# One V slot, a one-pair loop, o turned by the head sums, and thirty small loads in a decode block

## The chip, the cores and the metric

One core of a Trainium2 chip runs the kernel in one launch. The time is device time in microseconds (us). TensorE (PE) does matrix products, VectorE (DVE) and ScalarE (ACT) do elementwise work and reductions, GpSimd (POOL) helps VectorE, and SyncE (SP) issues nearly all transfers, on one queue; 16 DMA engines carry them out.

## The reference: what is computed

A decode step for 2 tokens: layer norm, attention with 32 heads over a cache of 8192 keys and values per head (float32, 128 wide), and a channel-mixing MLP (512 to 1792 to 512).

```python
q = (x @ wq).reshape(B, Sq, H, Dh)...            # x: layer-normed, [2, 1, 512]
scores = jnp.einsum("bhqd,bhkd->bhqk", q, k_cache) * (Dh ** -0.5)
p = _softmax(scores, axis=-1)
o = jnp.einsum("bhqk,bhkd->bhqd", p, v_cache)
h = x + o...reshape(B, Sq, H * Dh) @ wo
h2 = h + gelu(_layernorm(h) @ w1 + b1) @ w2 + b2
```

K and V are 2 x 32 x 8192 x 128 floats each, 268 MB each: nearly all of the 561 MB that the kernel loads, each byte used once.

## The kernel before, in words

**Units and pairs.** A pair g is two heads (16 pairs); a unit is one pair for one token b, so there are 32 units, and unit i = 2g + b. An even unit is the first token of its pair, an odd unit the second. A unit has a K tile and a V tile of 128 partitions x 16384 floats, 8.39 MB each: one half of the partitions for each head, 128 keys per partition.

**What one unit does.** K is multiplied in place by q, which stands broadcast in PSUM, in two chunks of 80 and 48 keys (`multiply`, VectorE); GpSimd folds the products of the first chunk in half (`halve`); VectorE sums them (`add_up`) and takes each partition's maximum (`row_max`). After the odd unit the pair's maxima are brought together (`all_max`), ScalarE computes the exponentials and their sums (`exps`), and TensorE multiplies them with V: `values` for the even V at the end of the odd unit, and for the odd V inside the next even unit. ScalarE copies the sum out (`gather`), and `head_sum` and `head_out` bring it into the form that the output projection needs. So the even V of a pair can only be used when both K tiles of that pair are done.

**Slots and the order of the loads.** Three slots of 8.39 MB (`slot`, a ring) hold all K and V tiles in turn, a new tile always taking the one longest unused. In unit i SyncE issues the V of unit i-1 and then the K of unit i+1 (`load`, L437). A load waits until what was in its slot has been read: V of unit j takes the slot of K of unit j, and K of unit j that of V of unit j-3. SyncE issues in order, so a load that waits holds up all behind it.

**Waits.** `Waits` follows every instruction by the memory that it reads and writes and gives each the semaphore waits that it needs. DMAs are put on 12 semaphores in turn (`LANES`); a DMA waits for the last one on its semaphore. `Rounds` writes TensorE's program of three pairs once and loops over it five times (`GH = 3`, L239 in the profile), the last pair being written out (L191).

**q.** Every third pair, `stage` copies the q of three pairs to partitions 0 to 3 (L417); `make_q` broadcasts one pair's q to 128 partitions in one of three PSUM banks.

**o.** Before, `head_sum` leaves 4 rows of 128 for each pair, `head_out` (L543) scales them into `orow`, which holds three pairs, and after every third pair `turn` transposes these 12 small pieces on TensorE and `turned` adds them into `oall`. The last pairs' o are laid out over 64 partitions chosen by `LEFT`, to fit a part of wo (`wog`) that GpSimd gathers row by row. In the last unit `project_all` multiplies all but the last pair with wo, while the last V is still loading; the last pair and the MLP follow at the end. Seventy-two small matmuls (`SPARE`) run at the start and their result is not used.

Of the kernel before, what the change touches and what calls it, by code (L numbers as in the profile page):

```python
# [12 lines left out]
P = 128  # L13
# [7 lines left out]
SPARE = 72  # L21
GP = 6
GH = 3
SR = 4
LW = 6
LEFT = (((3, 7), (9, 16), (20, 28), (44, 47), (54, 57), (67, 93), (101, 106), (110, 114), (118, 122)),)
# [12 lines left out]
class Waits:  # L39
    LANES = 12  # L40

    def __init__(self, nc):
        self.nc = nc
        self.sems, self.count, self.clock, self.after, self.mem, self.mask = ({} for _ in range(6))
        self.lane = {}
        self.off = False
        nc.push_inst_callback(self.seen)
# [63 lines left out]
    def skip(self, n):  # L111
        self.lane["hard"] += n
# [5 lines left out]
    def place(self, eng, op, areas):  # L118
        areas = [(x, w) for x, w in areas if x is not None]
        queue = (eng,)  # L120
        if "DMA" in op:
            kind = "soft" if eng == "Pool" else "hard"
            k = self.lane.get(kind, 0)
            self.lane[kind] = k + 1
            proc = (kind, k % self.LANES)
        else:
            proc = queue
# [33 lines left out]
    def close(self):  # L161
# [3 lines left out]
        last = ("hard", (self.lane["hard"] - 1) % self.LANES)  # L165
# [80 lines left out]
class Room:  # L246
# [3 lines left out]
    def tile(self, shape, dtype, name, tag=None, bufs=None, ahead=0):  # L250
# [6 lines left out]
        ring.append(ring.pop(ahead))  # L257
        v = ring[-1][:shape[0], :n]
# [6 lines left out]

    def turn(self, key, n):
        ring = self.held[key]
        ring[:] = ring[n:] + ring[:n]


def tile_decode_block(nc, waits, x, k, v, wq, wo, wog, w1, bias, w2, out):
# [10 lines left out]
    GL = NP - 1  # L282
    units = [(g, b) for g in range(NP) for b in range(B)]
# [11 lines left out]
    def slot():  # L295
        return kv.tile([P, ROW], F32, name="kv", tag="kv")
# [7 lines left out]
    wqt = slot()  # L304
# [3 lines left out]
    wgt = wts.tile([P, len(LEFT), SR, D], F32, name="wgt")  # L308
# [8 lines left out]
    orow = const.tile([4, GH, 2, DH], F32, name="orow")  # L317
    oall = const.tile([P, 2, 2 * GP, B], F32, name="oall")
    NQ = len(LEFT)
    og = const.tile([P, NQ * SR + LW - TH, B], F32, name="og")  # L320
    slots = [kept(x) for x in LEFT]
    first_slot = [sum(n for _, n in slots[:q]) for q in range(len(LEFT))]
    HG = H - LW
    NS = (HG - 4 * GP) * DH // SR
    assert sum(n for _, n in slots) == NS
# [3 lines left out]
    pms = {}  # L329
    for x in LEFT:  # L330
        if x not in pms:
            pms[x] = const.tile([P, P], F32, name=f"pm{len(pms)}")
            nc.gpsimd.memset(pms[x], 0.0)
            for p0, s0, n in kept(x)[0]:
                nc.gpsimd.tensor_copy(pms[x][:, p0:p0 + n], ident[:, s0:s0 + n])
    pm = [pms[x] for x in LEFT]
    FAR = 4096.0
    ioff = const.tile([P, len(LEFT)], F32, name="ioff")
    for q in range(len(LEFT)):
        nc.gpsimd.tensor_scalar(ioff[:, q:q + 1], pidx, first_slot[q] - FAR, None, op0=ALU.add)  # L340
# [9 lines left out]
    so2 = [psa.tile([P, 512], F32, name="so"), [psq.tile([P, 512], F32, name="qps") for _ in range(3)][2]]  # L350
# [5 lines left out]
    qs = const.tile([2 * B, GH, DH], F32, name="qs")  # L356
    wz = const.tile([P, B], BF16, name="wz")
    nc.gpsimd.memset(wz, 0.0)
# [9 lines left out]
    y2 = wgt[:B, 0, 0, :]  # L368
    nc.vector.tensor_scalar(y2, x2, mv[:, 0:1], rs, op0=ALU.subtract, op1=ALU.mult)

    ypt = psm.tile([P, DC, B], F32, name="sm")
# [4 lines left out]
    ipt = psm.tile([P, len(LEFT)], F32, name="sm")  # L376
    for q in range(len(LEFT)):
        pe.matmul(ipt[:, q:q + 1], pm[q], ioff[:, q:q + 1], start=True, stop=True)
# [8 lines left out]
    i4 = ident[:4, :4].rearrange("m (b s) -> m b s", s=2)  # L387
    hmask = const.tile([4, 2], F32, name="hmask")
    nc.vector.tensor_add(hmask, i4[:, 0, :], i4[:, 1, :])

    gidx = const.tile([P, len(LEFT)], mybir.dt.int32, name="gidx")
# [13 lines left out]
    QP, S, MX, MT, GM, LT, RL, SS, OP, OT, TP = ({} for _ in range(11))  # L405
# [5 lines left out]
    def stage(m):  # L411
        g = GH * min(m, NP // GH - 1) + 1
        n = next((n for n in range(1, GH) if (g + n) % NG == 0), 1)
        for at, n in ((0, n), (n, GH - n)):
            rows, cols = of_pair(g + at)
            src = q2[rows, cols.start:cols.start + n * DH]
            nc.vector.tensor_reduce(qs[:, at:at + n].rearrange("m k d -> m (k d)"), src[:, :, None], axis=AX.X, op=ALU.max)  # L417

    def make_q(g):
        QP[g] = psq.tile([P, B, DH], F32, name="qps")  # L420
        for b in range(B):
            rows, cols = of_pair(g)
            q = qs[:, (g - 1) % GH, :] if g else q2[rows, cols]
            pe.matmul(QP[g][:, b], pick[:2 * B, b, :], q, start=True, stop=True)

    make_q(0)
    stage(0)
    rowacc = psa.tile([B, D], F32, name="rowacc")
    for _ in range(SPARE):
        pe.matmul(rowacc[:, :B], wz, wz, start=True, stop=True)  # L430

    def load(src, i, parts):
        g, b = units[i]
        t = slot()
        rows = src[b, 2 * g:2 * g + 2].rearrange("h (p j) d -> (h p) (j d)", j=NS2)
        for s0, n in parts:
            nc.sync.dma_start(t[:, s0 * DH:(s0 + n) * DH], rows[:, s0 * DH:(s0 + n) * DH])  # L437
        return t

    def load_wo():  # L440
        t = slot()
        n = (2 * 2 * GP + LW) * D
        t = t[:, ROW - n:]
        nc.sync.dma_start(t, wo)
        for q in range(NQ):
            nc.gpsimd.indirect_dma_start(
                out=wgt[:, q].rearrange("p r n -> p (r n)"), out_offset=None,
                in_=wog,
                in_offset=bass.IndirectOffsetOnAxis(ap=gidx[:, q:q + 1], axis=0),
                bounds_check=NS - 1, oob_is_err=False)  # L450
        tv = t[:, :2 * 2 * GP * D].rearrange("p (j r n) -> p j r n", j=2, n=D)
        return tv, t[:, 2 * 2 * GP * D:].rearrange("p (r n) -> p r n", n=D)

# [24 lines left out]
    def row_max(i):  # L478
        g, b = units[i]
        if not b:  # L480
            MX[g] = work.tile([P, B], F32, name="mx", bufs=3)
            MT[g] = psm.tile([1, B, P], F32, name="sm")
# [3 lines left out]
    def all_max(g):  # L486
        gm = work.tile([1, B, 2], F32, name="gm", bufs=3)
        nc.vector.tensor_reduce(gm, MT.pop(g).rearrange("o b (s p) -> o b s p", s=2), axis=AX.X, op=ALU.max,  # L488
                                negate=True)
        GM[g] = psm.tile([P, B, 2], F32, name="sm")  # L490
# [15 lines left out]
    def total(g):  # L506
        RL[g] = psm.tile([4, 1] if g < GL else [P, 4], F32, name="sm")
        if g < GL:
            pe.matmul(RL[g], lt4, ones[:, 0:1], start=True, stop=True)
        else:  # L510
            pe.matmul(RL[g], ones, lt4, start=True, stop=True)

    def inverse(g):
        r = work.tile(list(RL[g].shape), F32, name="rl" if g < GL else "rlp")
# [17 lines left out]
    def head_sum(g):  # L532
        ss = SS.pop(g)
        OP[g] = psm.tile([4, DH] if g < GL else [P, 2 * B], F32, name="sm")
        for j in range(4):
            sj = ss[:, j * DH:(j + 1) * DH]
            a, w = (sel4[:, :, j], sj) if g < GL else (sj, sel4[:, :, j])
            pe.matmul(OP[g], a, w, start=(j == 0), stop=(j == 3))

    def head_out(g):  # L540
        op, rl = OP.pop(g), RL.pop(g)
        if g < GL:
            nc.vector.scalar_tensor_tensor(orow[:, g % GH], op[:, None, :].to_broadcast([4, 2, DH]), rl,  # L543
                                           hmask[:, :, None].to_broadcast([4, 2, DH]), op0=ALU.mult, op1=ALU.mult)
            return
        nc.vector.tensor_tensor(otz[:, :, 0:B], *(x.rearrange("p (b s) -> p s b", b=B) for x in (op, rl)),
                                op=ALU.mult)

    def turn(j):
        rows = orow.rearrange("m k e d -> m (k e d)")  # L550
        if j < 4:
            TP[j] = psm.tile([HP, 2 * GP, 2 * B], F32, name="sm")
            rows = rows.rearrange("m (p r) -> m r p", r=2 * GP)
            for r in range(2 * GP):
                pe.transpose(TP[j][:, r, :], rows[:, r, :], ident[:4, :4])
            psm.turn("sm", 2)
            return
        TP[j] = psm.tile([P, NQ * SR + LW - TH, 2 * B], F32, name="sm")
        at, n = (HG - 4 * GP) * DH, LW - TH
        last = rows[:, at:at + n * DH].rearrange("m (p r) -> m r p", r=n)  # L560
        for r in range(n):
            pe.transpose(TP[j][:, NQ * SR + r, :], last[:, r, :], ident[:4, :4])
        rows = rows.rearrange("m (s r) -> m r s", r=SR)
        for q, (_, n) in enumerate(slots):
            s0 = first_slot[q]
            for r in range(SR):
                pe.transpose(TP[j][:n, q * SR + r, :], rows[:, r, s0:s0 + n], ident[:4, :4])

    def turned(j):
        if j < 4:  # L570
            tp = TP.pop(j)
            half = slice(HP * (j % 2), HP * (j % 2 + 1))
            nc.vector.tensor_reduce(oall[half, j // 2], tp.rearrange("p r (b s) -> p r b s", b=B), axis=AX.X, op=ALU.add)
            return
# [271 lines left out]
```

## Time and profile before

| | |
|---|---|
| time, median of 2 runs | 1302.81 us (1302.77 to 1302.85) |
| profiled execution, first to last instruction | 1301.3 us (no other time of it is given) |
| bytes loaded | 561 MB, at 431 GB/s over the span |
| busy: VectorE, TensorE, GpSimd, ScalarE | 75%, 30%, 28%, 4% |
| SyncE's queue, share of the 16 engines' time | 99.7% |

The profile is one execution on the chip. A line of a timeline gives start and length in us, engine, line of the kernel, operation and what it writes and reads; brackets give the idle time ahead and what ended it. "SPq" is SyncE's queue: its entries are the moments at which a load is issued, not when it runs. The loads of K and V go by the tensor `kv` for all slots. In a table by windows each engine has its busy time and, in brackets, its instructions.

### The profile page before, as it was taken

To read this page: it belongs to the slowest core of one execution; us is meant where nothing else is said; L and a number is where in the kernel's file an instruction comes from. 1 tells how busy PE (TensorE), PEld (TensorE's weight loads), DVE (VectorE), ACT (ScalarE), POOL (GpSimd) and SP (SyncE) were. 2 spreads that over 40 slices of the span, in tenths; PEclk is the share of its full clock that TensorE was granted. 3 is DMA by queue.
4 is the path that set the end of the run, shared out by engine and by line. 5 is a ranking of instruction groups with operands and counts; after the bars stand their busy time and mean duration, and the time that the engine had idled before them with its cause. 6 is when DMAs were issued, how large, how long until landed. Compare 5 with 4: busy or idle time off the path is not lost.

```text
span 1301.3 us, 6543 instructions
## 1 busy us (share of the span) xinstructions
PE 384.8 (30%) x2890; PEld 118.5 (9%) x2890; DVE 976.5 (75%) x291; ACT 49.3 (4%) x157; POOL 366.5 (28%) x67
## 2 busy tenths in 40 slices
PE   3105023230412314033330513323032331502359
PEld 0001000000100001010000101001010100100113
DVE  1988777779777779777779877778877778977752
ACT  0000000000000000000000000000000000000011
POOL 1433311333321333321233331233331133332320
PEclk9556566575666657566665666657566665756669
DMA  9999999999999999999999999999999999999998
GB/s 404 435 449 422 445 420 445 424 434 435 429 439 431 437 427 441 425 441 429 429 441 429 437 433 437 421 445 425 435 435 431 437 433 437 423 445 423 437 427 375
DMA packets 10824, 561.17 MB, mean 431 GB/s; under 512 B 1398, under 2 KB 1398, under 8 KB 1660
## 3 DMA queue, kind: packets, MB, share of 16 engines
q1 hardware_dynamic: 10664, 560.48, 99.7%
q0 software_dynamic: 144, 0.52, 0.1%
q8 instruction: 8, 0.13, 0.0%
q14 instruction: 4, 0.03, 0.0%
q10 hardware_dynamic: 4, 0.00, 0.0%
HBM read 561.53 MB, written 0.00 MB: 432 GB/s over the span
## 4 chain that ended last, share of the span: by engine, by line
DMA 45%; DVE 40%; PE 13%; ACT 1%; issue 1%; POOL 0%; SPq 0%; another core or an unknown queue 0%
DMA kv<-in_k_dram 40%; DVE kv L468 22%; DVE s L476 15%; PE so L239 10%; DMA kv<-in_w_dram 3%; DMA kv<-in_wq_dram 2%; PE sm L239 1%; ACT pt L503 1%; PE so L191 1%; DVE gm L488 0%; DVE orow L543 0%; DVE mx L483 0%; POOL kv L472 0%; DVE qs L417 0%; DVE nb L496 0%
## 5 line engine op out<-in xcount | busy, mean ns | idle before, releaser
L468 DVE TENSOR_TENSOR kv<-kv,qps 128x10240 f32<-128x10240 f32 (+1 forms) x68 | 555.5, 8171 | 238.5 <-DMA kv<-in_k_dram 238.3
L472 POOL TENSOR_TENSOR kv<-kv 128x5120 f32<-128x5120 f32 (+1 forms) x36 | 358.2, 9951 | 878.9 <-DVE kv L468 463.5
L476 DVE TENSOR_REDUCE s<-kv 128x48 f32<-128x6144 f32 (+1 forms) x68 | 380.6, 5636 | 1.2 <-POOL kv L472 0.3
L239 PE MATMUL so<-kv,pt 128*16 128x512 f32 x1920 | 275.8, 739 | 254.9 <-DMA kv<-in_v_dram 234.1
L239 PE MATMUL sm<-ident,mx 128*1 128x128 f32 x30 | 9.7, 325 | 583.2 <-DVE mx L483 583.2
L239 PEld LDWEIGHTS so<-kv,pt 128*16 128x16 f32 x1920 | 61.4, 113 | 444.4 <-DMA kv<-in_v_dram 235.6
L239 PEld LDWEIGHTS sm<-ident,mx 128*1 128x1 f32 x30 | 2.4, 79 | 589.4 <-DVE mx L483 586.7
L503 ACT ACTIVATE pt<-s,nb 64x128 f32<-64x128 f32 x64 | 25.5, 399 | 663.1 <-DVE nb L496 661.9
L530 ACT ACTIVATE ss<-so 128x512 f32<-128x512 f32 x16 | 9.6, 597 | 540.6 <-PE so L239 503.3
L239 PE MATMUL sm<-ss,sel 128*4 128x128 f32 x120 | 15.6, 272 | 12.5 <-ACT ss L530 12.5
L191 PE MATMUL qps<-kv,pt 128*16 128x512 f32 x128 | 17.0, 692 | 7.1 <-DMA kv<-in_v_dram 7.1
L403 DVE COPY q<-so 128x512 f32<-128x512 f32 x1 | 0.7, 692 | 19.3 <-PE so L191 19.3
L515 DVE RECIPROCAL rlp<-sm 128x4 f32<-128x4 f32 x1 | 0.2, 183 | 18.3 <-PE sm L191 18.3
L191 PE MATMUL qps<-kv 128*32 128x128 f32 (+2 forms) x178 | 13.2, 296 | 0.2 <-DMA kv<-in_w_dram 0.2
L488 DVE TENSOR_REDUCE gm<-sm 1x4 f32<-1x256 f32 x16 | 6.6, 413 | 7.3 <-PE sm L239 7.0
L239 PEld LDWEIGHTS sm<-ss,sel 128*4 128x4 f32 x120 | 9.3, 87 | 28.2 <-ACT ss L530 17.3
L191 PE MATMUL so<-kv,yT 128*4 128x512 f32 x64 | 8.5, 691 | 11.5 <-DMA kv<-in_wq_dram 11.5
L503 ACT ACTIVATION_READ_ACCUMULATOR pt<-s,nb 64x1 f32 x64 | 11.8, 185 | 0.0
L239 PE MATMUL qps<-qs,pick 4*128 4x128 f32 x60 | 11.1, 306 | 0.0
L239 PE MATMUL sm<-gm,srow 1*128 1x4 f32 x30 | 8.7, 359 | 7.6 <-DVE gm L488 7.6
L191 PE MATMUL so<-kv,oall 128*2 128x512 f32 x48 | 7.7, 805 | 8.7 <-DMA kv<-in_wo_dram 8.7
L496 DVE COPY nb<-sm 128x4 f32<-128x4 f32 x15 | 2.4, 162 | 10.1 <-PE sm L239 10.1
(121 smaller groups left out, 124.4 us busy)
## 6 DMA issues: line engine op xcount, KB each, us to landing
kv<-in_k_dram SPq DMA_DIRECT2D x2, 4096.0 KB, 36.4
kv<-in_wo_dram SPq DMA_DIRECT2D x1, 7680.0 KB, 28.2
kv<-in_v_dram SPq DMA_DIRECT2D x1, 6144.0 KB, 27.9
kv<-in_w_dram SPq DMA_DIRECT2D x1, 3584.0 KB, 35.9
kv<-in_v_dram SPq DMA_DIRECT2D x1, 2048.0 KB, 28.5
kv<-in_w_dram SPq DMA_DIRECT2D x1, 1792.0 KB, 39.8
kv<-in_w_dram SPq DMA_DIRECT2D x1, 1024.0 KB
kv<-in_w_dram SPq DMA_DIRECT2D x1, 512.0 KB, 42.6
```

The costliest lines, as they stand in the source:

```text
L191: getattr(self.nc.tensor, what)(*aps, **how)
L239: ins = getattr(pe, what)(*aps, **how)
L403: nc.vector.tensor_copy(q2, so2[0])
L468: nc.vector.tensor_tensor(kc, kc, QP[g][:, b, None, :].to_broadcast([P, chunks(i)[c], DH]), op=ALU.mult)
L472: nc.gpsimd.tensor_tensor(kc[:, :, 0:HP], kc[:, :, 0:HP], kc[:, :, HP:DH], op=ALU.add)
L476: nc.vector.tensor_reduce(S[i][:, a:z], chunk(i, c, t)[:, :, 0:n], axis=AX.X, op=ALU.add)
L488: nc.vector.tensor_reduce(gm, MT.pop(g).rearrange("o b (s p) -> o b s p", s=2), axis=AX.X, op=ALU.max, negate=True)
L496: nc.vector.tensor_copy(nb, GM.pop(g))
L503: nc.scalar.activation(ptz[b][q, :, 4 * m:4 * m + 4], s[q], AF.Exp, bias=nb[q, b, e:e + 1], scale=SCALE, accum_out=lt4[q, m:m + 1])
L515: nc.vector.reciprocal(r, RL[g])
L530: nc.scalar.activation(SS[g], so2[g == GL], AF.Copy)
```

## The change

K tiles take turns in slots 0 and 1, every V tile goes to slot 2, and the last V to slot 1. TensorE's loop holds one pair and runs 15 times. PSUM banks are named instead of taken in turn: q always has the same one. `stage` copies one pair's q in each even unit. `head_sum` uses the gathered sum as the stationary side, so that o comes out turned, and `head_out` writes it to `oall`; `turn` and `turned` are gone, and `spread_out` lays two heads out over the 64 partitions at the end. wo is laid out to suit; its bytes are the same. DMA semaphores are 4, with separate ones for the late loads and the marks. `SPARE` is gone. `mark` issues fifteen loads of 1 to 15 rows of 64 bytes on SyncE's queue, in unit 4 and in unit 30; nothing reads what they load.

```diff
-    def slot():
-        return kv.tile([P, ROW], F32, name="kv", tag="kv")
+    def slot(at):
+        return kv.tile([P, ROW], F32, name="kv", tag="kv", at=at)
...
     def load(src, i, parts):
         g, b = units[i]
-        t = slot()
+        t = slot(i % 2 if src is k or i == NU - 1 else 2)
...
-    def stage(m):
...
+    def stage(g):
+        rows, cols = of_pair(min(g, NP - 1))
+        nc.vector.tensor_reduce(qs, q2[rows, cols][:, :, None], axis=AX.X, op=ALU.max)
...
     def make_q(g):
-        QP[g] = psq.tile([P, B, DH], F32, name="qps")
+        QP[g] = psq.tile([P, B, DH], F32, name="qps", at=0)
...
-    for _ in range(SPARE):
-        pe.matmul(rowacc[:, :B], wz, wz, start=True, stop=True)
...
     def total(g):
+        RL[g] = bank([P, 2 * B], 2)
+        pe.matmul(RL[g], ones, lt4, start=True, stop=True)
...
     def head_sum(g):
         ss = SS.pop(g)
+        OP[g] = bank([P, 2 * B], 1)
         for j in range(4):
+            pe.matmul(OP[g], ss[:, j * DH:(j + 1) * DH], sel4[:, :, j], start=(j == 0), stop=(j == 3))
 
     def head_out(g):
+        to = oall[:, 2 * g:2 * g + 2, :] if g < GL else otz[:, :, 0:B]
+        nc.vector.tensor_tensor(to, *(x.rearrange("p (b s) -> p s b", b=B) for x in (OP.pop(g), RL.pop(g))),
                                 op=ALU.mult)
...
+    def spread_out():
+        TP[0] = bank([P, 2, 2 * B], 2)
+        for h in range(2):
+            pe.matmul(TP[0][:, h], pm[:, h], oall[:, GA:GA + 2, :].rearrange("p s b -> p (s b)"),
+                      start=True, stop=True)
...
+    marks = const.tile([16, 2, 15, 16], F32, name="marks")
+
+    def mark(at):
+        for n in range(1, 16):
+            nc.sync.dma_start(marks[:n, at, n - 1], wq[:n, 16 * n:16 * n + 16])
...
     for i, (g, b) in enumerate(units):
         if i == NU - 1:
+            waits.late(12)
+            wot = load_wo()
         if i >= 1:
             VT[i - 1] = load(v, i - 1, full)
         if i + 1 < NU:
             KT[i + 1] = load(k, i + 1, full)
+        if i in (4, NU - 2):
+            waits.late(15, f"mark{i}")
+            mark(i // (NU - 2))
+            waits.late(4, "hard")
...
-        if b == 0 and g % GH == 0 and g < GL:
+        if b == 0 and g < GL:
             pe.round()
```

More of the change, by code (lines that the diff above doesn't have):

```diff
@@ L316, in tile_decode_block @@
     nc.gpsimd.memset(lt4, 0.0)
[L317 to L325, printed above, removed]
+    oall = const.tile([P, H - TH, B], F32, name="oall")
+    og = const.tile([P, SR, B], F32, name="og")
+    runs, ns = kept(LEFT)
+    assert ns == 2 * DH // SR == HP
     pidx = const.tile([P, 1], F32, name="pidx")
     nc.gpsimd.iota(pidx, pattern=[[0, 1]], base=0, channel_multiplier=1, allow_small_or_imprecise_dtypes=True)
[L329 to L336, printed above, removed]
+    pm = const.tile([P, 2, P], F32, name="pm")
+    nc.gpsimd.memset(pm, 0.0)
+    for p0, s0, n in runs:
+        nc.gpsimd.tensor_copy(pm[:, :, p0:p0 + n],
+                              ident.rearrange("p (h s) -> p h s", h=2)[:, :, s0:s0 + n])
     FAR = 4096.0
-    ioff = const.tile([P, len(LEFT)], F32, name="ioff")
-    for q in range(len(LEFT)):
-        nc.gpsimd.tensor_scalar(ioff[:, q:q + 1], pidx, first_slot[q] - FAR, None, op0=ALU.add)
+    ioff = const.tile([P, 1], F32, name="ioff")
+    nc.gpsimd.tensor_scalar(ioff, pidx, -FAR, None, op0=ALU.add)
     eps2 = const.tile([P, 1], F32, name="eps2")
@@ L349, in tile_decode_block @@
     nc.vector.memset(srow, SCALE)
-    so2 = [psa.tile([P, 512], F32, name="so"), [psq.tile([P, 512], F32, name="qps") for _ in range(3)][2]]
+    so2 = [psa.tile([P, 512], F32, name="so"), psq.tile([P, 512], F32, name="qps", at=2)]
     for t in so2:
@@ L374, in tile_decode_block @@
     nc.vector.tensor_copy(yT[:, :, B:2 * B], ypt)
-    ipt = psm.tile([P, len(LEFT)], F32, name="sm")
-    for q in range(len(LEFT)):
-        pe.matmul(ipt[:, q:q + 1], pm[q], ioff[:, q:q + 1], start=True, stop=True)
+    ipt = bank([P, 1], 1)
+    pe.matmul(ipt, pm[:, 0], ioff, start=True, stop=True)
     sel = const.tile([P, 16], F32, name="sel")
@@ L386, in tile_decode_block @@
                           sel[:, :2 * B].rearrange("p (s b) -> p b s", b=B)[:, :, :, None].to_broadcast([P, B, 2, HP]))
[L387 to L391, printed above, removed]
+    gidx = const.tile([P, 1], mybir.dt.int32, name="gidx")
     nc.vector.tensor_scalar(gidx, ipt, FAR, None, op0=ALU.add)
@@ L403, in tile_decode_block @@
     nc.vector.tensor_copy(q2, so2[0])
-    QP, S, MX, MT, GM, LT, RL, SS, OP, OT, TP = ({} for _ in range(11))
+    QP, S, MX, MT, GM, RL, SS, OP, TP = ({} for _ in range(9))
     def of_pair(g):
@@ L409, in of_pair @@
         return slice(32 * n, 32 * n + 2 * B), slice(j * DH, (j + 1) * DH)
-    def stage(m):
[L412 to L417, printed above, removed]
+    def stage(g):
+        rows, cols = of_pair(min(g, NP - 1))
+        nc.vector.tensor_reduce(qs, q2[rows, cols][:, :, None], axis=AX.X, op=ALU.max)
     def make_q(g):
-        QP[g] = psq.tile([P, B, DH], F32, name="qps")
+        QP[g] = psq.tile([P, B, DH], F32, name="qps", at=0)
         for b in range(B):
             rows, cols = of_pair(g)
-            q = qs[:, (g - 1) % GH, :] if g else q2[rows, cols]
-            pe.matmul(QP[g][:, b], pick[:2 * B, b, :], q, start=True, stop=True)
+            pe.matmul(QP[g][:, b], pick[:2 * B, b, :], qs if g else q2[rows, cols], start=True, stop=True)
     make_q(0)
-    stage(0)
+    stage(1)
     rowacc = psa.tile([B, D], F32, name="rowacc")
-    for _ in range(SPARE):
-        pe.matmul(rowacc[:, :B], wz, wz, start=True, stop=True)
     def load(src, i, parts):
         g, b = units[i]
-        t = slot()
+        t = slot(i % 2 if src is k or i == NU - 1 else 2)
         rows = src[b, 2 * g:2 * g + 2].rearrange("h (p j) d -> (h p) (j d)", j=NS2)
@@ L440, in load_wo @@
     def load_wo():
-        t = slot()
-        n = (2 * 2 * GP + LW) * D
-        t = t[:, ROW - n:]
+        t = slot(0)[:, ROW - (H - 2) * D:]
         nc.sync.dma_start(t, wo)
[L445 to L452, printed above, removed]
+        nc.gpsimd.indirect_dma_start(
+            out=wgt.rearrange("p r n -> p (r n)"), out_offset=None,
+            in_=wog,
+            in_offset=bass.IndirectOffsetOnAxis(ap=gidx, axis=0),
+            bounds_check=HP - 1, oob_is_err=False)
+        return t.rearrange("p (h n) -> p h n", n=D)
     def chunks(i):
@@ L480, in row_max @@
         if not b:
-            MX[g] = work.tile([P, B], F32, name="mx", bufs=3)
-            MT[g] = psm.tile([1, B, P], F32, name="sm")
+            MX[g] = work.tile([P, B], F32, name="mx", bufs=1)
+            MT[g] = bank([1, B, P], 0)
         nc.vector.tensor_reduce(MX[g][:, b:b + 1], S[i], axis=AX.X, op=ALU.max)
@@ L486, in all_max @@
     def all_max(g):
-        gm = work.tile([1, B, 2], F32, name="gm", bufs=3)
+        gm = work.tile([1, B, 2], F32, name="gm", bufs=1)
         nc.vector.tensor_reduce(gm, MT.pop(g).rearrange("o b (s p) -> o b s p", s=2), axis=AX.X, op=ALU.max,
                                 negate=True)
-        GM[g] = psm.tile([P, B, 2], F32, name="sm")
+        GM[g] = bank([P, B, 2], 1)
         pe.matmul(GM[g], srow, gm, start=True, stop=True)
@@ L506, in total @@
     def total(g):
[L507 to L511, printed above, removed]
+        RL[g] = bank([P, 2 * B], 2)
+        pe.matmul(RL[g], ones, lt4, start=True, stop=True)
     def inverse(g):
-        r = work.tile(list(RL[g].shape), F32, name="rl" if g < GL else "rlp")
+        r = work.tile([P, 2 * B], F32, name="rl")
         nc.vector.reciprocal(r, RL[g])
@@ L542, in head_out @@
[L542 to L546, printed above, removed]
-                                op=ALU.mult)
[L549 to L574, printed above, removed]
-        tp = TP.pop(j)
-        tp = tp.rearrange("p r (b s) -> p r b s", b=B)
-        for q, (_, n) in enumerate(slots):
-            at = slice(q * SR, (q + 1) * SR)
-            nc.vector.tensor_reduce(og[:n, at], tp[:n, at], axis=AX.X, op=ALU.add)
-        nc.vector.tensor_reduce(og[:, NQ * SR:], tp[:, NQ * SR:], axis=AX.X, op=ALU.add)
-        TP[j] = psm.tile([P, NQ * SR, B], F32, name="sm")
-        for q, (_, n) in enumerate(slots):
-            at = slice(q * SR, (q + 1) * SR)
-            pe.matmul(TP[j][:, at], pm[q][:n], og[:n, at], start=True, stop=True)
+        to = oall[:, 2 * g:2 * g + 2, :] if g < GL else otz[:, :, 0:B]
@@ L590, in project_all @@
+    def project_all(wot):
         so = so2[0]
[L591 to L593 removed]
+        parts = [(oall[:, h, :], wot[:, h, :]) for h in range(GA)]
+        parts += [(og[:, r, :], wgt[:, r, :]) for r in range(SR)]
+        parts += [(oall[:, h, :], wot[:, h - 2, :]) for h in range(GA + 2, H - TH)]
@@ L624, in tile_decode_block @@
                 elif b == 1:
-                    nc.vector.memset(orow, 0.0)
+                    nc.vector.memset(oall, 0.0)
                 if i == NU - 1:
-                    turn(4)
+                    spread_out()
             elif c == 1:
-                if b == 0 and g % GH == 1:
-                    turned(max(g // GH - 1, 0))
                 if i == NU - 1:
-                    turned(4)
+                    placed()
                 if b == 1 and g < GL:
                     make_q(g + 1)
-                    if g % GH == GH - 1:
-                        stage((g + 1) // GH)
             if c >= 1 and nch > 2:
@@ L660, in tile_decode_block @@
             total(g)
-            if g % GH == 0 and g < GL:
-                turn(max(g // GH - 1, 0))
     vlast = load(v, NU - 1, [(0, 96), (96, 32)])
-    wt = slot()
+    wt = slot(0)
     br = wt[:, 2 * DC * F:2 * DC * F + FN + P]
@@ L679, in tile_decode_block @@
     nc.scalar.activation(junk[:, 0:1], lt4[:, 0:1], AF.Sqrt)
-    late = slot()
+    late = slot(2)
     at = [0]
@@ L801, in _laid_out @@
     d = wo.shape[1]
-    rows = 4 * GP * P
-    last = len(wo) - LW * P
-    own = last + (LW - TH) * P
+    heads = wo.reshape(-1, P, d)
+    at = len(heads) - LW - 2
+    plain = _np.concatenate([heads[:at], heads[at + 2:]])
+    some = heads[at:at + 2].reshape(2, 2, HP, d).transpose(2, 1, 0, 3)
     halves = (_NG, 32, 2, len(b1) // (64 * _NG))
@@ L814, in _laid_out @@
         "wq": inputs["A_wq"],
-        "wo": _np.concatenate([wo[:rows].reshape(2, P, -1).transpose(1, 0, 2).reshape(P, -1),
-                               wo[last:own].reshape(P, -1),
-                               wo[own:].reshape(TH, P, d).transpose(1, 0, 2).reshape(P, -1)], axis=1),
-        "wog": wo[rows:last].reshape(-1, SR * d),
+        "wo": plain.transpose(1, 0, 2).reshape(P, -1),
+        "wog": some.reshape(HP, -1),
         "w1": w1,
```

68 lines of the change are left out of this document (27 added, 41 removed).

## The prediction

> **What bounds the kernel now.** I read the page's slices and queue shares first, then the chain of waits, the windows of single pairs, the waits of SyncE's queue, and last the timeline of one pair.
>
> ```profile
> span 1301.3 us, 6543 instructions
> PE 384.8 (30%) x2890; PEld 118.5 (9%) x2890; DVE 976.5 (75%) x291; ACT 49.3 (4%) x157; POOL 366.5 (28%) x67
> DMA  9999999999999999999999999999999999999998
> GB/s 404 435 449 422 445 420 445 424 434 435 429 439 431 437 427 441 425 441 429 429 441 429 437 433 437 421 445 425 435 435 431 437 433 437 423 445 423 437 427 375
> q1 hardware_dynamic: 10664, 560.48, 99.7%
> ```
>
> No compute engine is full (VectorE, the busiest, is at 75%), but the DMA engines work in every slice and SyncE's queue q1 fills 99.7% of them. The kernel takes as long as its loads. Whatever is done elsewhere costs nothing until it lets that queue run dry. The page gives no time of the profiled execution beside its span; the median of the two runs, 1302.81 us, is 1.5 us over the span, and I add that 1.5 at the end.
>
> The windows of two whole pairs (four loads of 8.39 MB each: K, V, K, V) give the pace:
>
> ```profile
> core 0: us, PE busy (x) PEld busy (x) DVE busy (x) ACT busy (x) POOL busy (x), PEclk, DMA share, GB/s
> 62.80:140.20 77.40, 22.63 (x162) 7.28 (x160) 60.33 (x16) 2.56 (x9) 22.07 (x2) 0.61 1.00 433
> 488.50:565.90 77.40, 22.04 (x150) 6.06 (x142) 60.04 (x14) 2.56 (x9) 22.07 (x2) 0.63 1.00 434
> ```
>
> A pair takes 77.40 us, two loads take 38.70 and one 19.35, with a DMA share of 1.00. Now one pair from the timeline (start, length, engine), which carries the whole argument:
>
> ```profile
> 480.24 0.33 SPq L437 DMA_DIRECT2D kv<-in_v_dram  x1
> 488.54 10.82 DVE L468 TENSOR_TENSOR kv<-kv,qps 128x10240 f32<-128x10240 f32 x1 [6.29 <-DMA kv<-in_k_dram]
> 492.10 0.33 SPq L437 DMA_DIRECT2D kv<-in_k_dram  x1
> 507.90 9.94 PE L239 MATMUL so<-kv,pt 128*16 128x512 f32 x64 [15.94 <-DMA kv<-in_v_dram]
> 517.88 0.33 SPq L437 DMA_DIRECT2D kv<-in_v_dram  x1
> 518.26 0.44 SPq L437 DMA_DIRECT2D kv<-in_k_dram  x1
> 519.62 0.08 PEld L239 LDWEIGHTS sm<-ident,mx 128*1 128x1 f32 x1 [0.22 <-issue]
> 519.82 0.71 PE L239 MATMUL qps<-qs,pick 4*128 4x128 f32 x4
> 527.23 10.82 DVE L468 TENSOR_TENSOR kv<-kv,qps 128x10240 f32<-128x10240 f32 x1 [9.06 <-DMA kv<-in_k_dram]
> 537.97 0.47 DVE L543 SCALAR_TENSOR_TENSOR orow<-sm,rl,hmask 4x256 f32<-4x256 f32 x1
> 556.90 0.33 SPq L437 DMA_DIRECT2D kv<-in_v_dram  x1
> 556.91 0.29 DVE L483 TENSOR_REDUCE mx<-s 128x1 f32<-128x128 f32 x1
> 560.10 9.44 PE L239 MATMUL so<-kv,pt 128*16 128x512 f32 x64 [1.39 <-ACT pt L503]
> 565.93 10.82 DVE L468 TENSOR_TENSOR kv<-kv,qps 128x10240 f32<-128x10240 f32 x1 [7.02 <-DMA kv<-in_k_dram]
> 569.68 0.33 SPq L437 DMA_DIRECT2D kv<-in_k_dram  x1
> ```
>
> K tiles land at 488.54, 527.23 and 565.93, where VectorE stops waiting for them. Call the one at 527.23 the odd K of pair g: its even K is at 488.54, and 565.93 is the even K of the next pair. When the odd K lands, VectorE multiplies and sums it until 557.2 (the maximum at 556.91 is the last step); then come the exponentials, and at 560.10 TensorE starts on the even V of the pair, which has lain in its slot all that time, and is done at 569.54. At 569.68 SyncE issues a K load: it reuses that V's slot. The even V of a pair is therefore held until 42.45 us (569.68 less 527.23) after the odd K has landed, while the queue needs only 38.70 us to move the next two loads. Today this does no harm, because the odd V was already issued at 556.90, once its slot (that of the odd K) was free, and it is in flight until 565.93 + 19.35 = 585.3.
>
> The chain of waits follows the same loop, and gives the mean over the pairs (by line, then its first and last piece of 15, from the issue of that K to its landing):
>
> ```profile
> by line: DMA kv<-in_k_dram 40.4%; DVE kv L468 22.3%; DVE s L476 15.5%; PE so L239 10.4%; DMA kv<-in_w_dram 3.3%; DMA kv<-in_wq_dram 1.7%; PE sm L239 1.3%; ACT pt L503 1.1%; PE so L191 0.7%; issue 0.5%; DVE gm L488 0.5%; DVE orow L543 0.4%;
> 105.53 34.65 DMA kv<-in_k_dram
> 1188.56 35.64 DMA kv<-in_k_dram
> ```
>
> 40.4% of 1301.3 is 525.7 us, over 15 pieces 35.05 each. Two loads back to back take 38.70, so this K is issued on average 3.65 us after the even K has landed (3.56 and 3.75 in the quoted pair), and 38.70 + 3.65 = 42.35 us after the odd one.
>
> **The change, V in one slot.** All V tiles but the last share slot 2, and K tiles take turns in slots 0 and 1. The order on SyncE's queue stays: odd V, odd K of the next pair, even V, even K. What each waits for moves:
>
> The odd V now waits for TensorE to have finished the even V of its pair, so it is issued where the K was, 42.35 us after the odd K's landing, and no longer 29.7 us after it (556.90). It stands one load earlier in the queue than the K that has this wait today. When it is issued the even K of the next pair has already landed and nothing is queued behind. That is the step on which the forecast rests: the queue stands empty once per pair. Behind the waiting V on SyncE's queue is only the next odd K, which follows at once and so lands later by the same.
>
> The even V waits for the odd V of the pair before: landing at 507.90, done at 517.84, and today's issue at 517.88 is at the same place, with the odd K in flight until 527.23. No pause there. Each K waits for VectorE's work on the K two units before it, over long before. So one pause per pair, at the odd V of pairs 0 to 14: 15 pauses. The last V goes to slot 1 and waits as today.
>
> **What the pause costs.** Of the 42.35 us something is taken off by the smaller head output, which stands between the two multiplications of the odd K: 0.47 us (537.97) becomes a product on 128x4, for which the same operation of the last pair stands below at 0.16. The copy of q (L417, two in 0.61 us, for three pairs) leaves odd units, where five of them held two copies: 5 x 0.61 / 15 = 0.20 per pair. The issue then comes at 42.35 - 0.31 - 0.20 = 41.84, that is 3.14 us after the queue has run dry.
>
> ```profile
> 0.74 0.39 SPq L305 DMA_DIRECT2D kv<-in_wq_dram  x1
> 22.69 8.49 PE L191 MATMUL so<-kv,yT 128*4 128x512 f32 x64 [11.51 <-DMA kv<-in_wq_dram]
> 1164.24 0.61 DVE L417 TENSOR_REDUCE qs<-q 4x128 f32<-4x128 f32 x2
> 1277.61 7.06 PE L191 MATMUL qps<-kv,pt 128*16 128x512 f32 x64
> 1286.96 0.16 DVE L546 TENSOR_TENSOR kv<-sm,rlp 128x4 f32<-128x4 f32 x1 [10.06 <-PE sm L191]
> out_dram<-kv SPq DMA_DIRECT2D x1, 4.0 KB, 1.4
> 1254.71 1.85 SPq L676 DMA_DIRECT2D kv<-in_w_dram  x4
> 1188.56 0.33 SPq L437 DMA_DIRECT2D kv<-in_k_dram  x1
> 1214.59 0.33 SPq L444 DMA_DIRECT2D kv<-in_wo_dram  x1
> ```
>
> A load on an empty queue costs more than 19.35: the load of wq, 8.39 MB like a K, finds the queue empty and takes 22.69 - 0.74 = 21.95 us, 2.60 more. The other bound is the store of the result, 4 KB issued to an idle queue and landed in 1.4 us. I take 2.60, since wq is the same transfer. So a pair loses 3.14 + 2.60 = 5.74 us, and 15 pairs 86.1. The fit in the Trainium skill ("DMA: Bandwidth & Descriptors", Anatomy of one DMA) has a fixed 2.0 us per DMA, measured on GpSimd's path; by it the pair would lose 5.14 and the sum be 77. The trace's 2.60 decides here.
>
> What spreads this: the shortest block on a V that the trace has is 7.06 us (TensorE warm, 1277.61) and the longest quoted 9.94, against 9.44; so a pair loses between 3.14 - 2.4 + 1.4 = 2.1 and 3.14 + 0.5 + 2.6 = 6.2 us, 32 to 94 in all.
>
> **The marks.** Fifteen loads, 120 rows of 64 bytes in all, behind K of unit 5 and again behind K of unit 31. Their issue, at 1.85 / 4 = 0.46 each, holds SyncE's queue 6.9 us. Behind the first set it holds V of unit 4, whose own wait ends some 26 us after that K was issued (492.10 to 517.88 today); behind the second the load of wo, also 26 us later (1188.56 to 1214.59). Both are covered. On the engines 7.7 KB is near the result's 4 KB: 1.4 us if a set runs together, 15 x 1.4 = 21 if each load ran alone; they add bytes and free nothing, so no gain. The first set lies after the K on which the next pause hangs, inside time that the pause leaves free up to 3.14 us: nothing. The second has no pause behind it: 1.4.
>
> **The rest goes at nothing.** The one-pair loop turns 15 times rather than 5, at the point where TensorE goes from the head sums to the transposed maxima; a turn stands in the quoted pair, with 0.22 us of idle (519.62), and after the q matmuls (to 520.5) TensorE waits until 557.2 for VectorE. One bank for q makes its matmuls (519.82) wait for VectorE's second multiplication of the odd K, 18 us after its landing; behind them on TensorE stands the transposed maximum, due at 29.7, so 11 us cover it. The turn of o through head sums, and one copy of q and the wider reciprocal in the even unit, lie on VectorE and TensorE where VectorE idles 6 to 9 us before each K. The 72 filler matmuls run at the start, before any K maximum. From the last odd K's landing to the end, loads, slots and bytes are the same.
>
> **Sum.** 1301.3 + 86.1 + 1.4 = 1388.8 us of span, with 1.5 around it 1390.
>
> **The rivals.**
> *The pause is made up.* The loads after a pause run faster, so the pair keeps 77.40 us: 1303 us plus the marks, 1304, no change. The four loads would have to take 71.7 us, 434 x 77.4 / 71.7 = 469 GB/s; to stay within 2% (26 us, 1.7 per pair) 458 decides. Against it: 433 and 434 in both windows, 449 in the highest slice. The Trainium skill agrees ("DMA: Bandwidth & Descriptors", Specifications): it puts the fabric's ceiling at 435 GB/s, so nothing could be made up. Chance 0.04.
> *The wait does not bind.* The change would not do what its diff says if TensorE's reads were over before the queue ran dry, by 36.1 us after the odd K's landing; 42.35 less the 2.4 of a wholly warm V block still is 40. Time 1303; chance 0.03.
> *Quick blocks and a cheap restart.* TensorE at full clock and 1.4 per restart: 15 x 2.1 = 32, time 1336. For it only the 7.06 of a TensorE warmed on purpose. Chance 0.04, slower still by 2.5%.
> *The marks run one by one.* 21 us a set, of which the first pause covers 3.1: 39 in all instead of 1.4, time 1428. Against it the 128 rows of the result within 1.4 us. Chance 0.04.
> Forecast: 0.85.
>
> **Numbers.** About 2% is what a measurement of this kernel can tell from no change. Slower by over 2%: 0.85 + 0.04 + 0.04 = 0.93; within it 0.04 + 0.03 = 0.07 from the first two rivals, of which I give 0.02 to faster, for a gain that no row shows. The range reaches down to a restart of 1.4 (15 x 1.2 = 18 less) with V blocks 0.3 us shorter on average (5 less), 1367, and up to the longest block in every pair (15 x 0.5 = 7 more) with marks that run together only in part (6 more), 1403. The rivals, 0.15 together, stay outside.
>
> **What would show it.** Slices with a DMA share below 0.95 in every pair, and about 403 GB/s over a pair (433.5 x 77.4 / 83.1); SyncE's odd V issued 3 us after a K landed, waiting for TensorE; K landings 38.7 and 44.4 us apart in turn; VectorE idle 9.06 + 5.74 = 14.8 us before odd Ks. If the windows still show 434 GB/s, the step with the empty queue is wrong; if the pause is there and is not 5.7 us, the restart is mis-sized; if the time goes up with landings 38.7 apart, it is the marks.

## The result, and the profile after

The changed kernel takes 1391.62 us (two runs, 1391.11 and 1392.14) against 1302.81: 1.068 times the time of before, 95% interval 1.066 to 1.070. That is 88.8 us slower, where 87.2 were forecast. The profiled execution took 1391.11 us, 1.3 more than its span.

The page of the changed kernel, the rows that answer to those of before:

```profile
span 1389.8 us, 6332 instructions
DMA  9989979999998989989799898989989899998998
GB/s 408 438 363 423 451 334 423 392 423 424 390 423 362 423 377 434 426 362 451 334 453 423 362 445 370 423 362 423 451 364 423 362 451 394 385 430 362 420 436 354
q1 hardware_dynamic: 11144, 560.50, 94.1%
```

The bytes are the same, but SyncE's queue fills 94.1% of the engines' time instead of 99.7%, and the missing part comes back about once per pair (a pair is 2.4 slices): slices at 334 to 394 GB/s stand between slices at 420 and more. The windows of two pairs, from one even K to the next:

```profile
core 0: us, PE busy (x) PEld busy (x) DVE busy (x) ACT busy (x) POOL busy (x), PEclk, DMA share, GB/s
517.10:600.10 83.00, 21.26 (x158) 6.87 (x154) 60.12 (x16) 2.56 (x9) 22.04 (x2) 0.63 0.94 404
1015.30:1098.20 82.90, 21.40 (x154) 6.86 (x150) 60.12 (x15) 2.56 (x9) 22.05 (x2) 0.63 0.94 405
```

VectorE's, ScalarE's and GpSimd's work per pair is what it was (60 us on VectorE), TensorE's is a little less. Only the loads are spread over 83 us instead of 77.4. The first of these pairs in the timeline:

```profile
510.92 8.91 PE L235 MATMUL so<-kv,pt 128*16 128x512 f32 x64 [1.39 <-ACT pt L473]
517.07 10.82 DVE L438 TENSOR_TENSOR kv<-kv,qps 128x10240 f32<-128x10240 f32 x1 [7.33 <-DMA kv<-in_k_dram]
519.97 0.33 SPq L411 DMA_DIRECT2D kv<-in_v_dram  x1
520.34 0.43 SPq L411 DMA_DIRECT2D kv<-in_k_dram  x1
542.05 8.71 PE L235 MATMUL so<-kv,pt 128*16 128x512 f32 x64 [21.90 <-DMA kv<-in_v_dram]
550.91 0.33 SPq L411 DMA_DIRECT2D kv<-in_v_dram  x1
561.40 10.82 DVE L438 TENSOR_TENSOR kv<-kv,qps 128x10240 f32<-128x10240 f32 x1 [14.23 <-DMA kv<-in_k_dram]
572.14 0.15 DVE L507 TENSOR_TENSOR oall<-sm,rl 128x4 f32<-128x4 f32 x1
578.81 1.22 PE L235 MATMUL qps<-qs,pick 4*128 4x128 f32 x4 [26.06 <-DVE kv L438]
591.11 0.37 PE L235 MATMUL sm<-ident,mx 128*1 128x128 f32 x1 [11.08 <-DVE mx L453]
600.08 10.82 DVE L438 TENSOR_TENSOR kv<-kv,qps 128x10240 f32<-128x10240 f32 x1 [7.31 <-DMA kv<-in_k_dram]
602.45 0.33 SPq L411 DMA_DIRECT2D kv<-in_v_dram  x1
```

The even K lands at 517.07 and nothing is queued behind it. TensorE ends its block on the even V at 519.83 (510.92 and 8.91), SyncE issues the odd V at 519.97, and TensorE can use it at 542.05, 22.08 us after its issue. The next odd K lands at 561.40, 44.33 after the even one instead of 38.70, and VectorE has idled 14.23 us before it. From there to the next even K it is 38.68 again. The waits of SyncE's queue name the same cause (source and what was waited for, total us, times, longest). The first line is the longest of before, and it names VectorE; the other two are the longest of after:

```profile
SPq L437 <- DVE mx L483: 968.2, 31, 39.3
SPq L411 <- PE sm L235: 763.4, 15, 53.2
SPq L411 <- PE so L235: 420.0, 15, 30.6
```

All 30 waits for a V slot now end with TensorE; the 15 of the row with `sm` are the pauses.

The packet records of the trace show what a pause is made of in this pair. The 16 engines end their last rows of the even K at 516.26 us on average, 0.8 before VectorE goes on, and start on the odd V at 521.26, 1.3 after its issue. So each stands idle for 5.0 us, and its first row of the V takes 2.99 us instead of 2.42: together 5.6, by which the odd K is late.

### The profile page after: what moved, and what is told of

The parts are those of the page before. It is cut to its first block, busy times and chain, and to the rows that moved or that the text cites. A ratio compares the mean times of both kernels' runs of the same rounds, so it can differ in the third digit from the quotient of the medians.

```text
span 1389.8 us, 6332 instructions
## 1 busy us (share of the span) xinstructions
PE 380.4 (27%) x2752; PEld 122.5 (9%) x2752; DVE 972.6 (70%) x287; ACT 49.2 (4%) x157; POOL 366.2 (26%) x66
## 3 DMA queue, kind: packets, MB, share of 16 engines
q1 hardware_dynamic: 11144, 560.50, 94.1%
## 4 chain that ended last, share of the span: by engine, by line
DMA 51%; DVE 34%; PE 13%; ACT 1%; issue 0%; POOL 0%; SPq 0%
DMA kv<-in_k_dram 42%; DVE kv L438 20%; DVE s L446 14%; PE so L235 10%; DMA kv<-in_w_dram 3%; DMA kv<-in_wo_dram 3%; DMA kv<-in_wq_dram 2%; DMA kv<-in_v_dram 2%; PE sm L235 1%; PE so L187 1%; ACT pt L473 1%; DVE gm L458 0%; POOL kv L442 0%; DVE mx L453 0%; DVE nb L466 0%
## 5 line engine op out<-in xcount | busy, mean ns | idle before, releaser
L235 PE MATMUL so<-kv,pt 128*16 128x512 f32 x1920 | 268.1, 722 | 347.9 <-DMA kv<-in_v_dram 327.1
L235 PE MATMUL qps<-qs,pick 4*128 4x128 f32 x60 | 18.3, 456 | 380.8 <-DVE kv L438 380.8
L235 PEld LDWEIGHTS qps<-qs,pick 4*128 4x128 f32 x60 | 13.9, 318 | 384.0 <-DVE kv L438 384.0
L235 PE MATMUL sm<-sel,ss 128*128 128x4 f32 x120 | 15.8, 255 | 12.1 <-ACT ss L497 12.1
L235 PEld LDWEIGHTS sm<-sel,ss 128*128 128x128 f32 x120 | 14.5, 191 | 25.9 <-ACT ss L497 25.9
L482 DVE RECIPROCAL rl<-sm 128x4 f32<-128x4 f32 x16 | 2.8, 176 | 19.0 <-PE sm L187 19.0
```

The lines of the kernel that those rows point to most:

```text
L235: ins = getattr(pe, what)(*aps, **how)
L482: nc.vector.reciprocal(r, RL[g])
```

## The experiments

The theory: SyncE's queue runs dry once per pair, because the odd V waits until TensorE has read the whole even V, and a load on a dry queue needs some 2.6 us more. The rivals: the thirty small loads hold up the engines; or TensorE's new program (the one-pair loop, the single bank of q, the turn of o) costs the time.

**One V slot alone.** The kernel before, with only the slots changed.

```diff
-        t = slot()
+        t = slot(i % 2 if src is k or i == NU - 1 else 2)
```

> The kernel before with nothing changed but the slots: K in slots 0 and 1 in turn, V in slot 2, the last V in slot 1; three-pair loop, o transposed as before, no marks. Pause theory (SyncE's queue runs dry once per pair because the odd V waits until TensorE has read the whole even V): the pair loses 3.65 us of waiting, with no shorter head output, and 2.60 of restart, 15 x 6.25 = 94: 1397 us, between 1385 and 1400. Marks theory (the thirty small loads hold the engines up) and TensorE theory (the one-pair loop, the single bank of q or the new turn of o cost the time): 1303 us, no change.

Measured: 1397.89 us, 1.073 times (1.071 to 1.075). This one line brings the whole loss, and 6 us more than the full change, close to what was worked out from the longer head output and the copies of q that stay in odd units: the odd V is issued 3.40 us after the even K on average of 14 pairs, where the full change has 2.81. One pair of its timeline:

```profile
520.53 10.82 DVE L469 TENSOR_TENSOR kv<-kv,qps 128x10240 f32<-128x10240 f32 x1 [6.25 <-DMA kv<-in_k_dram]
524.00 0.33 SPq L438 DMA_DIRECT2D kv<-in_v_dram  x1
566.43 10.82 DVE L469 TENSOR_TENSOR kv<-kv,qps 128x10240 f32<-128x10240 f32 x1 [16.26 <-DMA kv<-in_k_dram]
```

**The ring put back.** The changed kernel with the three slots in turn, and so three pairs in the loop.

```diff
-        return kv.tile([P, ROW], F32, name="kv", tag="kv", at=at)
+        return kv.tile([P, ROW], F32, name="kv", tag="kv")
...
-        if b == 0 and g < GL:
+        if b == 0 and g % 3 == 0 and g < GL:
             pe.round()
```

> The changed kernel with the three slots taken in turn again, as before; TensorE's loop then has to hold three pairs. The single bank of q, o turned by the head sums, the four semaphores and the marks stay. Pause theory: 1303 us and the two sets of marks, which no pause covers now, 1.4 to 1.7 us each: 1306 us. Marks theory: 1390 us, as the changed kernel. TensorE theory: 1390 us if the turn of o or the bank costs the time, and if it is the number of loop turns, 1303 us plus a third of the difference.

Measured: 1306.38 us, 1.0027 times (1.0016 to 1.0038). The turn of o, the single bank of q and the four semaphores stay in this kernel and cost nothing; the 3.6 us over the kernel before are the marks, as the next run shows. Its window over a pair, with the columns as above:

```profile
488.50:565.90 77.40, 22.53 (x146) 6.86 (x142) 60.13 (x15) 2.56 (x9) 22.07 (x2) 0.60 1.00 434
```

**The marks alone, and the change without them.** Fifteen small loads twice, added to the kernel before (its loads stay on 12 semaphores); and taken from the changed kernel.

```diff
+        if i in (4, NU - 2):
+            waits.late(15, f"mark{i}")
+            mark(i // (NU - 2))
+            waits.late(12, "hard")
```

> The kernel before with nothing added but the two sets of fifteen small loads. Pause theory: there is no pause to cover the first set, so both count: 1.4 to 1.7 us each, 1306 us. Marks theory: 1340 to 1390 us.

> The changed kernel without its thirty small loads. Pause theory: only the second set lies on the path: 1391.6 - 1.4 = 1390 us. Marks theory: 1303 us, or at least 40 us less than the changed kernel if each small load runs by itself.

Measured: added to the kernel before 1306.41 us, 1.0028 times (1.0017 to 1.0039), so 3.6 us for both sets (the K behind the first lands 0.8 late in the trace); without them the change takes 1389.38 us, 2.2 less than with them. Its runs spread from 1387.43 to 1391.42, so that the time alone doesn't carry the 2.2; the trace does. In the changed kernel the first set delays the K behind it, and the next pause takes the delay in:

```profile
188.86 5.30 SPq L536 DMA_DIRECT2D marks<-in_wq_dram  x15
229.17 10.82 DVE L438 TENSOR_TENSOR kv<-kv,qps 128x10240 f32<-128x10240 f32 x1 [15.09 <-DMA kv<-in_k_dram]
269.53 10.82 DVE L438 TENSOR_TENSOR kv<-kv,qps 128x10240 f32<-128x10240 f32 x1 [9.00 <-DMA kv<-in_k_dram]
270.79 0.33 SPq L411 DMA_DIRECT2D kv<-in_v_dram  x1
```

The even K lands 40.36 us after the odd one, 1.66 late, and the odd V is then issued only 1.26 us after it, where a pause has 2.8 on average. The second set lies on the path: the load of wo is used 20.24 us after the last odd K (1331.28 less 1311.04), and 18.18 without marks (1328.26 less 1310.08).

```profile
1311.04 4.42 DVE L438 TENSOR_TENSOR kv<-kv,qps 128x4096 f32<-128x4096 f32 x1 [15.68 <-DMA kv<-in_k_dram]
1331.28 6.61 PE L187 MATMUL so<-kv,oall 128*2 128x512 f32 x48 [30.45 <-DMA kv<-in_wo_dram]
```

```profile
1310.08 4.42 DVE L438 TENSOR_TENSOR kv<-kv,qps 128x4096 f32<-128x4096 f32 x1 [16.03 <-DMA kv<-in_k_dram]
1328.26 7.76 PE L187 MATMUL so<-kv,oall 128*2 128x512 f32 x48 [28.26 <-DMA kv<-in_wo_dram]
```

**Three pairs in the loop, one V slot.** Only the second part of the ring's diff.

> The changed kernel with three pairs in TensorE's loop instead of one, five turns instead of fifteen; slots, banks, o and marks as in the changed kernel. Pause theory: a turn lies where TensorE waits for VectorE anyway: 1391 us, within 3. If a turn of the loop cost the time, ten turns fewer would save two thirds of the 89 us: 1332 us.

Measured: 1394.51 us, 1.071 times (1.068 to 1.073). Ten turns of the loop fewer save nothing. The 2.9 us over the change stand in the pauses: the odd V is issued 3.05 us after the even K on average of 14 pairs, where the change has 2.81. Why it is later there stays open.

**A delay, in both kernels.** A sum on VectorE in the chain from the odd K to the odd V's issue, where the change has no slack and the kernel before has 15.7 us.

```diff
+        if b == 1 and g < GL:
+            nc.vector.tensor_reduce(idle2, idle1, axis=AX.X, op=ALU.add)
         row_max(i)
```

> The changed kernel with one sum over 4096 elements added on VectorE ahead of the maximum of each odd unit but the last (15 in all; by the rate of the sums in the profile, 11.95 us for two that read 128x6144 and 128x5120, about 4.3 us each); nothing reads its result. Pause theory: it lies on the path from the odd K's landing to the odd V's issue, so each pair loses it whole: 15 x 4.3 = 65 us, 1456 us. If the loads alone set the pace: 1391 us.

> The kernel before with the same sum added in the same place. Pause theory: the K load that waits for the even V's reading is issued with the odd V still in flight for 38.70 + 19.35 - 42.35 = 15.7 us, so 4.3 us more cost nothing: 1303 us. If VectorE's work is on the path in this kernel: 1367 us.

Measured: in the changed kernel 1455.45 us, 63.8 more than without it; the sum takes 4.41 us, 66 over 15 pairs. In the kernel before 1303.18 us, 1.0003 times (0.9991 to 1.0014): the same 66 us of work in the same place cost nothing. First the timeline of the changed kernel with the delay, then that of the kernel before with it:

```profile
789.60 4.41 DVE L593 TENSOR_REDUCE idle<-q 128x8 f32<-128x4096 f32 x1
799.03 10.82 DVE L438 TENSOR_TENSOR kv<-kv,qps 128x10240 f32<-128x10240 f32 x1 [3.12 <-DMA kv<-in_k_dram]
806.69 0.33 SPq L411 DMA_DIRECT2D kv<-in_v_dram  x1
848.59 10.82 DVE L438 TENSOR_TENSOR kv<-kv,qps 128x10240 f32<-128x10240 f32 x1 [19.45 <-DMA kv<-in_k_dram]
```

```profile
557.04 4.41 DVE L656 TENSOR_REDUCE idle<-q 128x8 f32<-128x4096 f32 x1
566.18 10.82 DVE L468 TENSOR_TENSOR kv<-kv,qps 128x10240 f32<-128x10240 f32 x1 [2.83 <-DMA kv<-in_k_dram]
573.93 0.33 SPq L437 DMA_DIRECT2D kv<-in_k_dram  x1
```

With one V slot the odd V is issued 7.66 us after the even K, and the odd K lands 49.56 after it. In the kernel before, the K that waits is issued 7.75 us after the even K, and that is harmless, since the odd V is in flight.

**The V in pieces.** The wait taken apart: with the V loaded in halves or quarters, a piece of the odd V waits only for that piece of the even V.

```diff
-            VT[i - 1] = load(v, i - 1, full)
+            VT[i - 1] = load(v, i - 1, [(j * NS2 // 4, NS2 // 4) for j in range(4)])
```

> The changed kernel with each V loaded in two halves, so that the first half of the odd V waits only for TensorE's reading of the first half of the even V, some 5.5 us of a block of 9 (TensorE runs slower at the start of a block); six semaphores instead of four. Pause theory: the first half is issued about 38.3 us after the odd K's landing, 0.4 before the queue is dry, and a restart that takes 2.6 then still loses 2.2 per pair: 33 us, 1338 us, between 1320 and 1345. If the restart is hidden as soon as the issue comes before the landing: 1306 us. Marks or TensorE theory: 1390 us.

> The changed kernel with each V loaded in four quarters, ten semaphores. The first quarter of the even V is read some 3.4 us after the block begins, so the odd V's first quarter is issued about 36.1 us after the odd K's landing, 2.6 before the queue would be dry; later quarters come free every 2 to 3 us, and a quarter takes 4.8 to move. Pause theory: no pause is left, 1303 us plus both sets of marks: 1306 us, between 1303 and 1312. Marks or TensorE theory: 1390 us.

Measured: halves 1339.8 us (1.028 times, 1.025 to 1.031), as expected to 2 us; quarters 1327.01 us (1.019, 1.015 to 1.022), 21 more than expected. In the timelines the first piece of the odd V is issued ahead of the even K's landing; first a pair with halves, then two with quarters:

```profile
500.81 3.76 SPq L411 DMA_DIRECT2D kv<-in_v_dram  x2
502.04 10.82 DVE L438 TENSOR_TENSOR kv<-kv,qps 128x10240 f32<-128x10240 f32 x1 [7.97 <-DMA kv<-in_k_dram]
542.12 10.82 DVE L438 TENSOR_TENSOR kv<-kv,qps 128x10240 f32<-128x10240 f32 x1 [9.98 <-DMA kv<-in_k_dram]
```

```profile
494.47 5.48 SPq L411 DMA_DIRECT2D kv<-in_v_dram  x4
497.35 10.82 DVE L438 TENSOR_TENSOR kv<-kv,qps 128x10240 f32<-128x10240 f32 x1 [7.55 <-DMA kv<-in_k_dram]
537.82 10.82 DVE L438 TENSOR_TENSOR kv<-kv,qps 128x10240 f32<-128x10240 f32 x1 [10.37 <-DMA kv<-in_k_dram]
574.10 6.50 SPq L411 DMA_DIRECT2D kv<-in_v_dram  x4
576.75 10.82 DVE L438 TENSOR_TENSOR kv<-kv,qps 128x10240 f32<-128x10240 f32 x1 [7.57 <-DMA kv<-in_k_dram]
615.86 10.82 DVE L438 TENSOR_TENSOR kv<-kv,qps 128x10240 f32<-128x10240 f32 x1 [9.00 <-DMA kv<-in_k_dram]
```

Issued 1.23 us before the even K lands, a half loses 40.08 - 38.70 = 1.38 us: the rule of the whole V, time of issue plus 2.6, still holds there. It holds on average too: over 14 pairs the first half is issued 0.72 us before the landing, and 1.88 us are lost. Issued some 2.7 before, quarters should lose nothing, and from an even K to the odd one they took 39.84 us on average of 14 pairs. The mean hides two kinds: seven pairs took 38.93 to 39.11 (39.11 at 576.75) and lost next to nothing, as forecast, and seven took 40.05 to 41.25 (40.47 at 497.35), at much the same time of issue. Two more runs bear on this.

**The price of cutting, and an earlier first piece.** Quarters with the ring put back; and, with one V slot, only the odd V cut, its first piece an eighth.

```diff
+            VT[i - 1] = load(v, i - 1, [(0, 16), (16, 24), (40, 40), (80, 48)] if b == 0 else full)
```

> The kernel with the slots taken in turn again (1306.4 us), with each V loaded in four quarters. It prices the cutting alone, with no wait on the path: in the kernel with one V slot and quarters, two loads without a wait between them took 38.93 us instead of 38.70, over 31 pairs of loads 7 us: 1313 us. If cutting costs nothing: 1306 us, and then all of the 1327 of the quartered kernel is waiting.

> The changed kernel with only the odd V cut, into 16, 24, 40 and 48 keys, so that its first piece waits for an eighth of TensorE's block and is issued about 4.2 us before the even K lands (the quarters came at 2.6 to 2.9 before and lost 0.9 us per pair on average). If that loss was the early engines running dry before the slowest has finished the even K: it goes, and 1303 us plus 3.6 for the marks and 3.5 for half of the cutting remain, 1310 us. If the loss comes from the cutting or from the later pieces: about 1320 us.

Measured: quarters in the ring 1314.51 us, 8.1 more than the ring with whole Vs, where 7 were expected. In its trace two loads take 38.93 us, so cutting costs 0.23 us for two loads with no wait about. The odd V in four uneven pieces: 1321.7 us (1.015 times, 1.013 to 1.017) where 1310 was expected, with the first piece issued 4.1 us or more before the even K lands. From an even K to the odd one it still took 39.58 us on average of 14 pairs. So the remainder, 0.7 to 0.9 us per pair, is not the first piece coming too late. Nor are the engines dry there. The window over two of these pairs has a DMA share of 1.00 with 429 GB/s against 434, and the window over all 14 pairs has 1.00 with 428:

```profile
493.70:650.00 156.30, 49.75 (x292) 14.35 (x288) 120.48 (x31) 5.12 (x18) 44.22 (x4) 0.62 1.00 429
```

The pages say the same by the share of SyncE's queue. In order: whole Vs in the ring (span 1305.4 us), the odd V in four pieces (1319.7), quarters in the ring (1313.5), quarters in one slot (1327.7).

```profile
q1 hardware_dynamic: 11144, 560.50, 99.5%
q1 hardware_dynamic: 17624, 560.50, 99.4%
q1 hardware_dynamic: 24536, 560.50, 99.6%
q1 hardware_dynamic: 24536, 560.50, 99.0%
```

Share times span gives, to about 1 us, the time for which the engines were busy. With the odd V in four pieces it is 1312 against 1299 us: nearly all of the 14 us over the ring is busy time, the same bytes moved more slowly, of which 3.5 is the estimate for the cutting. With quarters in one slot it is 1314 against 1308: about 6 of the 14 us over the ring with quarters are busy time and 8 are time with idle engines. Why the pieces move more slowly, and why half of the pairs with quarters lose nothing, stays open.

No kernel tried is faster than the one before, whose loads ran at 433 and 434 GB/s in both windows of a pair.

## Why the prediction was right

*The odd V waits for TensorE, once per pair.* Right: one line of the change, put alone into the kernel before, cost 95 us, and the ring put back took away all but the marks.

*The wait, 3.14 us after the queue has run dry.* Measured 2.81 on average over 14 pairs, from 1.26 (the pair behind the marks) to 3.96. In 11 of the pairs TensorE's block on the even V began 6.1 to 6.4 us before the even K landed, and the wait, 2.37 to 3.96, went with the length of the block: that of 8.46 us (at 344.59) had a granted clock of 0.50 for its first 2.9 us and 1.00 after, that of 9.97 us (at 925.22) for its first 5.9. The even Ks lie 83.1 us apart on average (14 pairs from 101.78 to 1265.25), where 83.14 was forecast.

*The restart, 2.60 us, read from wq's load.* Measured 44.21 - 38.70 - 2.81 = 2.70 on average, and 2.44 to 2.73 in 12 of the 14 pairs, whatever the wait. The row of wq was the right one to take; 1.4, the store's, would have put the time at 1372. The Trainium skill's fixed 2.0 us ("DMA: Bandwidth & Descriptors", Anatomy of one DMA) is for GpSimd's path and stands below what SyncE's queue shows here.

*No pause at the even V.* Right: issued at 550.91 with the odd K in flight until 561.40.

*The marks: nothing for the first set, 1.4 for the second.* The first delays a K by 1.66 us, and the pause behind it takes that in. The second costs 2.06, so the term was too small by 0.7. Uncovered, both sets cost 3.6 together.

*The work priced at nothing.* Right for the loop's turns, the single bank and the turn of o. The matmuls of q wait at 578.81 for VectorE, and the transposed maximum comes at 591.11 with 11.08 us of idle before it: the cover of 11 us that was named.

*The rivals.* The pause is not made up: the two loads after it took 38.68 us in the quoted pair and 38.90 on average, no less than before. The wait binds: in no pair was the odd V issued before the even K had landed. TensorE's blocks on the even V, where the timeline has them in one piece, took 8.46 to 9.97 us, not 7.06. The marks do not run one by one.

*The total, 1388.8 us of span, came out as 1389.8, and that it is so close is in part luck.* Errors cancel: the wait was 0.33 per pair too long, the restart 0.1 and the marks 0.7 too short, and 0.20 more per pair passed between odd and even Ks. In the last pair the odd K landed 45.79 us after the even one, with its V issued 2.57 after it: 4.5 us for the restart instead of 2.7. Without marks it was the same (46.14 and 2.88), so it is not the marks; what it is stays open.

## What to carry to other kernels

On a queue that is issued in order, count for every slot the time from the landing that starts its consumers to its release, and set it against the time that the loads already queued behind that landing will last: 42 against 38.7 us made 89 us here, while 42 against 58 had cost nothing, and 4.4 us more cost nothing either. The load that waits for the slow reader cost nothing where it was the K behind an odd V still in flight, and cost a pause where it was the odd V itself. The price of a dry queue here was the wait plus a restart, and a load of the same size that met an empty queue elsewhere in the same trace gave the restart to 0.1 us.

## What the runs showed of the hardware that was not expected

Two sets of fifteen loads, 15 KB in all, cost 3.6 us when nothing covers them, as much as 1.6 MB at 434 GB/s, and 5.3 us of SyncE's issue per set, 0.35 each. Quarters of an 8.39 MB load, with rows of 16 KB instead of 64, cost 0.23 us for two loads. Issuing the next load 2.6 to 4 us ahead of the landing did not bring back the whole loss: 0.7 to 0.9 us per pair stayed on average. With the odd V in four pieces nearly all of that was time in which the engines were busy, and why is unexplained.
